# Linear attention and two expert layers on one core: scores and values by key halves on four array tiles

## The chip, the cores and the metric

The kernel runs on one core of a Trainium2 chip. The metric is the time of one execution in device microseconds (us). The kernel before takes 1233.74 us, the median of three runs (1233.2 to 1234.08).

## The reference

Three stages follow each other on 3072 tokens (4 batches of 768) with 384 features.

```python
for t in range(S):                       # H = 8 heads of D = 48, S = 768
    state = alpha[:, :, t, :, None] * state + einsum('bhd,bhe->bhde', k[:, :, t], v[:, :, t])
    y[:, :, t] = einsum('bhd,bhde->bhe', q[:, :, t], state)
x = y as (tokens, 384)
h = x @ w_in                             # 384 -> 2048
x = where(h > 0, h, exp(min(h, 0)) - 1) @ w_out
p = domain_probs / (domain_probs.sum(-1) + 1e-9)
for e in range(4):                       # 384 -> 1024 -> 384
    out += p[:, e:e+1] * (relu(x @ w1[e]) @ w2[e])
```

## The kernel before

The attention is computed in chunks of C = 128 tokens; six chunks of four batches make 24 **units** (chunk, batch). With P the running product of the decays inside a chunk, q is multiplied by P and k by 1/P; the scores are then k times q, masked to the causal triangle, and the values are v times masked scores plus the state of the chunks before. A unit has these parts, each a function: `prep0` (the product P by a scan on VectorE, its logarithm and inverse on ScalarE), `prep1` (a Newton step for the inverse, which also scales k), `prep2` (scales q), `scores` (L439, and the masks L447 on VectorE), `ktrans` (four transposes of k, L460), `yout_t` (the states' share L485 and the values L490, then `pack`), `state` (the new state, L521 and two steps of VectorE) and `xtrans` (y into the operand x0 of the next layer, as a high and a low part: L547 on ScalarE, L548 on VectorE).

The heads stand two by two: head h uses the partitions 64 (h % 2) to 64 (h % 2) + 48 of `raw`, so two heads use the upper and the lower half of the array's rows (two **row tiles**). Scores have 128 columns of weights, so they run as two tiles. In L485 the weights are 64 wide and the output goes to partitions 0 or 64, so there are two **column tiles** as well, and four heads are in flight. In L490 the contraction is over all 128 keys and the output over 48 of 64 partitions: two column tiles. `pack` copies the two banks of y to SBUF (L499), and six small DMAs (L505) then move the last two heads' rows, 16 partitions each, to where the next layer wants them.

The first expert layer works on **items** (chunk, f), 16 for each chunk, 96 in all. An item has two halves of nine matmuls each: `first` computes 128 hidden features for 512 tokens (L620), and `second` feeds those of the item two before into three output banks (L645). Between them VectorE and ScalarE apply the activation: two activations of ScalarE (L629, L630), L631 on VectorE, a copy of ScalarE (L636) and L637 on VectorE. Behind each half a list `slots` places one step of a unit (and one of the weight preparation for the last layer, L547, L548, L673): the attention of chunk c runs during the items of chunk c - 1. The 24 steps of a chunk's four units are spread over 26 halves.

Work on other engines that depends on a half is put on a queue with `later` and issued by the next `flush`, of which there is one in each half. PE, ScalarE, VectorE and GpSimd run in exactly this order, SP's DMAs in an order that the scheduler sets. In each unit the steps come as

```python
s = [scores + ktrans], [prep0 of the next], [prep1 of the next], [xtrans of the one before],
    [yout_t + state], [prep2 of the next]
```

PSUM has eight banks. `a0` and `a1` serve scores and values in turn (`abank`), `h0` to `h2` the first halves, the transposes and the new states in turn (`hbank`), `t0` to `t2` the second halves. Chunks 1 and 2 run in a prologue with an order of its own and in the first items; the last layer (L924 on) begins at about 500 us.

## Time and profile before

| | |
|---|---|
| median of three runs | 1233.74 us (1233.2 to 1234.08) |
| the profiled execution | 1234.16 us |
| its span | 1232.5 us, 17874 instructions, mean granted clock 0.998 |
| PE busy | 1219.7 us (99%) |
| VectorE busy | 869.0 us (71%) |
| ScalarE busy | 592.8 us (48%) |
| GpSimd busy | 492.5 us (40%) |

A matmul's end is modelled, so busy PE is read as "PE was not idle", and the cost of a part is read from one start to the next. A wait behind a row in brackets is the idle time of the engine before it and what ended it. PEld is TensorE's weight load, which overlaps its matmuls.

### The profile page before, as it was taken

Reading aid. Unit: us, or ns where it says so; the run is one execution under the profiler, and the core shown is the slowest. Engines: PE = TensorE matmul, PEld = TensorE weight load, DVE = VectorE, ACT = ScalarE, POOL = GpSimd, SP = SyncE. Lnnn points to the kernel's source line nnn. Section 1 sums busy time; section 2 is a strip of 40 time slices with the busy share of each in tenths; the row PEclk is TensorE's granted clock in tenths of the full one; section 3 lists DMA queues with packets and bytes.
Section 4 is the critical chain, followed back from the end, with each engine's and each line's share of the span. In section 5 each row is a group of like instructions: output and inputs, shape, how many; then the busy total and the mean of one; then the engine's idle time right before and its main releaser. Section 6 shows DMA issues by size and latency. Waiting matters only on the chain.

```text
span 1232.5 us, 17874 instructions
## 1 busy us (share of the span) xinstructions
PE 1219.7 (99%) x6475; PEld 994.3 (81%) x6475; DVE 869.0 (71%) x1433; ACT 592.8 (48%) x1092; POOL 492.5 (40%) x388
## 2 busy tenths in 40 slices
PE   8999999999999999999999999999999999999997
PEld 5788888888887888788888888888888888888886
DVE  8996877777777678657576757575766576667664
ACT  6886566667666567434334333433433333342331
POOL 2000000000000000377688847867977474546662
PEclk9999999999999999999999999999999999999999
DMA  9632555555546467536556578654645874344331
GB/s 375 218 111 90 185 183 182 183 189 197 187 157 221 144 218 261 197 137 233 190 179 227 214 270 311 235 212 154 242 185 215 327 252 167 120 158 167 108 128 62
DMA packets 64816, 239.93 MB, mean 195 GB/s; under 512 B 7640, under 2 KB 33464, under 8 KB 55376
## 3 DMA queue, kind: packets, MB, share of 16 engines
q1 hardware_dynamic: 63856, 233.99, 52.9%
q10 hardware_dynamic: 864, 4.72, 1.0%
q8 instruction: 53, 0.87, 0.3%
q14 instruction: 43, 0.35, 0.1%
HBM read 178.27 MB, written 59.42 MB: 193 GB/s over the span
## 4 chain that ended last, share of the span: by engine, by line
PE 94%; DVE 4%; ACT 1%; DMA 0%; issue 0%; SPq 0%; ACTq 0%; DVEq 0%
PE h L924 27%; PE t L971 16%; PE t L645 16%; PE h L620 15%; PE a L971 11%; PE h L971 5%; PE a L439 2%; PE a L490 2%; PE a L485 1%; PE h L460 1%; PE h L521 1%; DMA raw<-in_att_dram 0%; DVE s_s L263 0%; DVE cv L93 0%; DVE s_p L220 0%
## 5 line engine op out<-in xcount | busy, mean ns | idle before, releaser
L944 POOL TENSOR_TENSOR u<-u 128x512 f32<-128x512 f32 x66 | 97.4, 1475 | 583.4 <-DMA pb<-pd 484.2
L924 PE MATMUL h<-xc_Q,wa 128*128 128x512 f32 x780 | 219.0, 390 | 0.2
L645 PE MATMUL t<-g,w_W 128*128 128x512 f32 x864 | 215.4, 393 | 0.0
L620 PE MATMUL h<-x,w_W 128*128 128x512 f32 x864 | 214.0, 392 | 1.2 <-DVE g L637 0.7
L899 ACT ACTIVATE g_W<-c 128x512 fp32r<-128x512 f32 x128 | 80.6, 630 | 276.4 <-DVE c L944 266.9
L944 DVE TENSOR_TENSOR u<-h,u 128x512 f32<-128x512 f32 x225 | 154.8, 688 | 80.8 <-PE h L924 79.8
L902 POOL TENSOR_TENSOR g_W<-c,g_W 128x512 fp32r<-128x512 f32 x128 | 165.5, 1301 | 77.1 <-ACT c L900 73.0
L620 PEld LDWEIGHTS h<-x,w_W 128*128 128x128 f32 x864 | 160.6, 188 | 35.8 <-DVE g L637 1.2
L645 PEld LDWEIGHTS t<-g,w_W 128*128 128x128 f32 x864 | 160.3, 188 | 33.9 <-issue 0.4
L924 PEld LDWEIGHTS h<-xc_Q,wa 128*128 128x128 f32 x780 | 145.9, 188 | 32.1 <-DVE c L944 0.8
L971 PE MATMUL t<-g_W,wb 128*128 128x512 f32 x576 | 157.5, 389 | 0.0
L900 ACT ACTIVATE c<-c 128x512 f32<-128x512 f32 x192 | 121.5, 633 | 12.2
L971 PEld LDWEIGHTS t<-g_W,wb 128*128 128x128 f32 x576 | 108.1, 188 | 22.5
L944 DVE TENSOR_TENSOR c<-u,h 128x512 f32<-128x512 f32 x123 | 84.2, 685 | 45.3 <-PE h L924 44.9
L631 DVE SCALAR_TENSOR_TENSOR h<-e,h 128x512 f32<-128x512 f32 x96 | 66.6, 693 | 66.1 <-ACT e L630 65.9
L938 DVE COPY u<-h 128x512 f32<-128x512 f32 x99 | 68.3, 691 | 59.2 <-PE h L924 59.1
L924 PE MATMUL h<-xc_W,wa 128*128 128x512 f32 x390 | 109.5, 389 | 0.0
L971 PE MATMUL a<-g_W,wb 128*128 128x512 f32 x384 | 108.2, 389 | 0.0
L899 ACT ACTIVATE g_X<-c 128x512 fp32r<-128x512 f32 x64 | 40.3, 629 | 132.1 <-DVE c L944 125.5
L902 POOL TENSOR_TENSOR g_X<-c,g_X 128x512 fp32r<-128x512 f32 x64 | 82.8, 1305 | 39.6 <-ACT c L900 35.5
L924 PEld LDWEIGHTS h<-xc_W,wa 128*128 128x128 f32 x390 | 73.0, 188 | 15.6 <-DVE u L944 0.4
L629 ACT ACTIVATE e<-h 128x512 f32<-128x512 f32 x96 | 57.2, 595 | 56.1 <-PE h L620 54.8
(162 smaller groups left out, 1789.0 us busy)
## 6 DMA issues: line engine op xcount, KB each, us to landing
wa<-wad SPq DMA_DIRECT2D x33, 1536.0 KB, 6.4
wb<-wbd SPq DMA_DIRECT2D x30, 1536.0 KB, 7.4
raw<-in_att_dram SPq DMA_DIRECT2D x22, 964.0 KB, 6.2
wad<-wh SPq DMA_DIRECT2D x44, 384.0 KB, 2.8
wbd<-wh SPq DMA_DIRECT2D x43, 384.0 KB, 3.3
xcd<-xh SPq DMA_DIRECT2D x30, 512.0 KB, 2.9
wraw<-in_we_dram SPq DMA_DIRECT2D x20, 576.0 KB, 4.4
xc_Q<-xcd SPq DMA_DIRECT2D x6, 1536.0 KB, 7.6
```

The costliest lines, as they stand in the source:

```text
L439: nc.tensor.matmul(ps[j][:, a * C:(a + 1) * C], raw[r, K0 + a * C:K0 + (a + 1) * C], raw[r, Q0 + a * C:Q0 + (a + 1) * C], start=True, stop ...
L620: nc.tensor.matmul(h[:, 0:n], w[:, wl, fi, k * 128:(k + 1) * 128], x[:, xl, k, n0:n0 + n], start=((k, wl, xl) == TERMS[0]), stop=((k, wl, ...
L629: nc.scalar.activation(out=e, in_=h, func=AF.Relu, scale=-1.0)
L631: return lambda: nc.vector.scalar_tensor_tensor(out=h, in0=e, scalar=-1.0, in1=h, op0=ALU.add, op1=ALU.max)
L645: nc.tensor.matmul(self.xa[k][:, 0:n], w[:, wl, fi, DM + k * 128:DM + (k + 1) * 128], g[:, gl, 0:n], start=(first and i == 0), stop=(last ...
L899: nc.scalar.activation(out=g[:, n, 0], in_=v, func=AF.Relu)
L900: nc.scalar.activation(out=v, in_=v, func=AF.Relu)
L902: lambda: nc.gpsimd.tensor_tensor(out=g[:, n, 1], in0=v, in1=g[:, n, 0].bitcast(F32), op=ALU.subtract)
L924: nc.tensor.matmul(b, w[:, wl], x[:, xl], start=(j == 0), stop=(j == 2))
L938: nc.vector.tensor_copy(out, b)
L944: (nc.vector if "b" in (a0, a1) or dst == "S5" else nc.gpsimd).tensor_tensor(out=out, in0=val(a0, b), in1=val(a1, b), op=ALU.add if op == ...
L971: nc.tensor.matmul(oa[m, d], wt[:, f, wl, d * 128:(d + 1) * 128], G[m][:, f, gl], start=first, stop=last)
```

## The change

From chunk 3 on (`TURNED = 2` counts chunks from 0), so for 16 of the 24 units:

- **Scores** are computed by halves of 64 keys. The early half meets all 128 queries, the late half only the last 64, since the others are masked away. Each matmul has 64 columns of weights, so four tiles are in use. In every second pair of heads the halves of k are exchanged (by the Newton step, which writes them so) and with them those of v (on the host), so that the two pairs of a round use different column tiles.
- **Masks**: three operations for each bank instead of one, into two tiles `smt` whose never-written corners are zeroed once by `begin_turned` on GpSimd, together with a second mask for the exchanged order.
- **Values** contract over 64 keys at a time, on four tiles. Row tile 0 writes bank `ps[0]`, row tile 1 `ps[1]`, the states' share as well; each head has a part in both. `pack` copies the first bank (one copy by ScalarE) and `total`, one flush later, adds the second on VectorE; the six DMAs start behind it.
- **Order** of a unit's steps: scores, transposes; prep0 and xtrans; prep1; values and state; prep2; an empty step.
- For all chunks `swap`, which gives the column tile of a head, follows another rule, with the rows of w_in exchanged to match, and `norm_probs` is spread over three items.

```diff
-    return h ^ (h // 2 % 2)
+    return h ^ ((h // 2 ^ h // 4) % 2)
...
+            kp = l if u[0] >= TURNED else k
             nc.vector.tensor_tensor(out=t, in0=P, in1=rP, op=ALU.mult)
-            nc.vector.tensor_tensor(out=k, in0=k, in1=rP, op=ALU.mult)
-            nc.vector.scalar_tensor_tensor(
-                out=k, in0=t, scalar=2.0, in1=k, op0=ALU.subtract, op1=ALU.mult, reverse0=True
-            )
+            nc.vector.tensor_tensor(out=kp, in0=k, in1=rP, op=ALU.mult)
+            parts = [(k, t, kp)]
+            if u[0] >= TURNED:
+                o, t, kp = (v.rearrange("p (a n) t -> p a n t", n=2) for v in (k, t, kp))
+                lo, hi = slice(0, 64), slice(64, C)
+                parts = [(o[:, :, 0], t[:, :, 0], kp[:, :, 0])]
+                parts += [(o[:, :, 1, i], t[:, :, 1, j], kp[:, :, 1, j]) for i, j in ((hi, lo), (lo, hi))]
+            for out, t, kp in parts:
+                nc.vector.scalar_tensor_tensor(
+                    out=out, in0=t, scalar=2.0, in1=kp, op0=ALU.subtract, op1=ALU.mult, reverse0=True
+                )
...
+        for a0 in (0, 2):
+            for late in range(2):
+                for a in (a0, a0 + 1):
+                    n, q = 64 * (late ^ a % 2), a * C + 64 * late
+                    for j in range(2):
+                        r = slice(64 * j, 64 * j + D)
+                        nc.tensor.matmul(
+                            ps[j][n:n + 64, q:(a + 1) * C], raw[r, K0 + a * C + n:K0 + a * C + n + 64],
+                            raw[r, Q0 + q:Q0 + (a + 1) * C], start=True, stop=True,
+                        )
...
+                for v in (
+                    (slice(0, 128), slice(None), slice(None), slice(64, C)),
+                    (slice(0, 64), slice(None), 0, slice(0, 64)),
+                    (slice(64, 128), slice(None), 1, slice(0, 64)),
+                ):
+                    nc.vector.tensor_tensor(out=o[v], in0=s[v], in1=m[v], op=ALU.mult)
...
+            if apart:
+                return ps[row][r:r + n, h // 2 * C:(h // 2 + 1) * C]
...
+            for late, order in enumerate((range(H), (0, 3, 4, 7, 1, 2, 5, 6))):
+                for h in order:
+                    row = late ^ h // 2 % 2
+                    other = row != h % 2
+                    r, q = slice(64 * row, 64 * row + 64), 64 * late * (not other)
+                    n = 64 if other and not swap(h) % 2 else D
+                    nc.tensor.matmul(
+                        to(h, n, row)[:, q:C], raw[r, V0 + h * D:V0 + h * D + n],
+                        self.sm[u, h % 2][r, h // 2, q:C], start=False, stop=True, skip_group_check=True,
+                    )
...
+            def total():
+                nc.vector.tensor_tensor(out=y[0:SW], in0=ps[1][0:SW], in1=y[0:SW], op=ALU.add)
+                spread()
+
+            if apart:
+                nc.scalar.copy(y[0:SW], ps[0][0:SW])
+                self.later(total)
...
+        if u[0] >= TURNED:
+            s[1:] = [s[1] + s[3], s[2], s[4], s[5], []]
...
-        at(F1 + 2, self.norm_probs)
+        for n in range(3):
+            at(F1 + n, self.norm_probs, n)
```

The line numbers move: L439 becomes L498 (scores), L447 becomes L514 (masks), L460 L523, L485 L552, L490 L563, L521 L611, L620 L712, L645 L737, L631 L723, L637 L729, L419 L450, L429 L460 (the product for q), L529 and L530 L619 and L620, L548 L638, L673 L765; the sum of the two banks is L586. In the rows of the order below the third word on names output and input tiles (`a` the score and value banks, `h` and `t` the layer's, `smt` and `sm` masked scores, `wc`, `ut` and `wh` the weight preparation) and the size of the output.

PE, the scores of the first unit of chunk 4, before and then in the change (the first nine of 17 rows there):

```order
L439 MATMUL a_2132<-raw 128x128
L439 MATMUL a_2133<-raw 128x128
L439 MATMUL a_2132<-raw 128x128
L439 MATMUL a_2133<-raw 128x128
L439 MATMUL a_2132<-raw 128x128
L439 MATMUL a_2133<-raw 128x128
L439 MATMUL a_2132<-raw 128x128
L439 MATMUL a_2133<-raw 128x128
L460 MATMUL h_2142<-ident,raw 128x128 x4
```

```order
L498 MATMUL a_2222<-raw 64x128
L498 MATMUL a_2223<-raw 64x128
L498 MATMUL a_2222<-raw 64x128
L498 MATMUL a_2223<-raw 64x128
L498 MATMUL a_2222<-raw 64x64
L498 MATMUL a_2223<-raw 64x64
L498 MATMUL a_2222<-raw 64x64
L498 MATMUL a_2223<-raw 64x64
L498 MATMUL a_2222<-raw 64x128
```

Eight matmuls of 128 rows and 128 columns of output become sixteen of 64 rows, four with 128 columns and four with 64 in turn.

PE, the same unit's states and values, before and then in the change (from the last row of the states):

```order
L485 MATMUL a_2233<-raw,st_146 64x128 x2
L485 MATMUL a_2234<-raw,st_146 64x128 x2
L485 MATMUL a_2233<-raw,st_146 64x128 x2
L485 MATMUL a_2234<-raw,st_146 64x128 x2
L490 MATMUL a_2233<-sm,raw 48x128 x2
L490 MATMUL a_2234<-sm,raw 48x128 x2
L490 MATMUL a_2233<-sm,raw 48x128 x2
L490 MATMUL a_2234<-sm,raw 48x128 x2
L521 MATMUL h_2251<-raw,kn 64x48 x8
```

```order
L552 MATMUL a_2316<-raw,st_146 64x128
L563 MATMUL a_2315<-smt,raw 48x128 x2
L563 MATMUL a_2316<-smt,raw 48x128 x2
L563 MATMUL a_2315<-smt,raw 48x128
L563 MATMUL a_2315<-smt,raw 64x128
L563 MATMUL a_2316<-smt,raw 64x128
L563 MATMUL a_2316<-smt,raw 48x128
L563 MATMUL a_2316<-smt,raw 64x128
L563 MATMUL a_2315<-smt,raw 64x128
L563 MATMUL a_2316<-smt,raw 48x128
L563 MATMUL a_2315<-smt,raw 48x128
L563 MATMUL a_2316<-smt,raw 48x64
```

Eight values of 128 columns become sixteen; the last four have 64 columns (the first of them is shown). The states stay eight.

VectorE, the same unit, from the last Newton step to the sum's place, before and then in the change:

```order
L419 SCALAR_TENSOR_TENSOR raw<-nt,raw 128x512
L637 TENSOR_TENSOR g<-h_2176,g 128x512
L548 TENSOR_TENSOR wh<-wc,wh 128x3x128
L673 TENSOR_TENSOR ut<-wraw 128x128
L673 TENSOR_TENSOR ut<-ut,wraw 128x128
L673 TENSOR_TENSOR wc<-ut,wraw 128x256
L673 TENSOR_TENSOR wc<-wc,wraw 128x128 x2
L631 SCALAR_TENSOR_TENSOR h_2215<-e,h_2215 128x512
L529 TENSOR_TENSOR tmp<-h_2251,st_146 128x192
L530 TENSOR_TENSOR st_146<-tmp,P 128x4x48
L429 TENSOR_TENSOR raw<-raw,P 128x512
L673 TENSOR_TENSOR wc<-wraw 128x256
```

```order
L450 SCALAR_TENSOR_TENSOR raw<-nt,lnP 128x2x64 x2
L729 TENSOR_TENSOR g<-h_2276,g 128x512
L638 TENSOR_TENSOR wh<-wc,wh 128x3x128
L619 TENSOR_TENSOR tmp<-h_2341,st_146 128x192
L620 TENSOR_TENSOR st_146<-tmp,P 128x4x48
L460 TENSOR_TENSOR raw<-raw,P 128x512
L765 TENSOR_TENSOR ut<-wraw 128x128
L765 TENSOR_TENSOR ut<-ut,wraw 128x128
L765 TENSOR_TENSOR wc<-ut,wraw 128x256
L765 TENSOR_TENSOR wc<-wc,wraw 128x128 x2
L723 SCALAR_TENSOR_TENSOR h_2352<-e,h_2352 128x512
L586 TENSOR_TENSOR yt<-a_2316,yt 112x512
```

The two steps of the state (`tmp`, `st`) and the product for q (`raw<-raw,P`) stood behind the activation's step of the item (L631) and stand ahead of it now (L723); the sum of the banks (L586) is new and stands right behind that step.

## Rows read from the trace of the kernel before

**Rows 1.** The page, busy us of each engine, share of the span, instructions

```profile
PE 1219.7 (99%) x6475; PEld 994.3 (81%) x6475; DVE 869.0 (71%) x1433; ACT 592.8 (48%) x1092; POOL 492.5 (40%) x388
```

**Rows 2.** Windows: stretch: length, busy (x instructions) by engine, clock, DMA share, GB/s

```profile
124.00:495.00 371.00, 370.76 (x2365) 301.54 (x2366) 281.57 (x552) 242.50 (x508) 0.00 (x0) 1.00 0.56 193
...
193.50:262.60 69.10, 69.10 (x507) 56.09 (x507) 53.84 (x105) 46.09 (x99) 0.00 (x0) 1.00 0.55 189
```

**Rows 3.** Timeline, PE, a unit of chunk 4: start us, length us, engine, line, operation

```profile
195.67 1.16 PE L439 MATMUL a<-raw 48*128 48x128 f32 x16
196.77 0.66 PE L460 MATMUL h<-ident,raw 128*128 128x128 f32 x4
...
205.55 0.67 PE L485 MATMUL a<-raw,st 48*64 48x128 f32 x16
206.14 1.08 PE L490 MATMUL a<-sm,raw 128*48 128x128 f32 x16
207.06 0.62 PE L521 MATMUL h<-raw,kn 128*64 128x48 f32 x16
...
209.79 2.21 PE L620 MATMUL h<-x,w_W 128*128 128x512 f32 x9
211.93 1.16 PE L439 MATMUL a<-raw 48*128 48x128 f32 x16
```

**Rows 4.** Windows with one start, L485 alone: (x) counts records that have started

```profile
205.50:205.73 0.23, 0.18 (x8) 0.18 (x12) 1.00 0.00 0
...
205.50:205.84 0.34, 0.29 (x12) 0.29 (x16) 1.00 0.00 0
```

**Rows 5.** The same for L521

```profile
207.00:207.11 0.11, 0.06 (x4) 0.11 (x4) 1.00 0.00 0
...
207.00:207.17 0.17, 0.12 (x6) 0.17 (x6) 1.00 0.00 0
```

**Rows 6.** Timeline, PE, a unit of the last chunk

```profile
367.76 0.67 PE L485 MATMUL a<-raw,st 48*64 48x128 f32 x16
...
369.37 0.50 PE L645 MATMUL t<-g,w_W 128*128 128x512 f32 x1
```

**Rows 7.** Groups by form, VectorE, 193.5 to 262.6: busy us, mean ns, idle before

```profile
L631 DVE SCALAR_TENSOR_TENSOR h<-e,h 128x512 f32<-128x512 f32 x14 | 9.7, 694 | 12.2 <-ACT e L630 12.2
...
L447 DVE TENSOR_TENSOR sm<-a,mask 128x512 f32<-128x512 f32 x8 | 5.1, 682 | 0.0
...
L673 DVE TENSOR_TENSOR wc<-wc,wraw 128x128 f32<-128x128 f32 x6 | 1.8, 292 | 0.2
...
L673 DVE TENSOR_TENSOR wc<-wraw 128x256 f32<-128x256 f32 x2 | 0.8, 418 | 0.0
```

**Rows 8.** Timeline, VectorE, the same unit

```profile
203.94 0.70 DVE L631 SCALAR_TENSOR_TENSOR h<-e,h 128x512 f32<-128x512 f32 x1 [2.31 <-ACT e L630]
...
206.47 0.68 DVE L637 TENSOR_TENSOR g<-h,g 128x512 fp32r<-128x512 f32 x1
...
207.54 0.28 DVE L673 TENSOR_TENSOR ut<-wraw 128x128 f32<-128x128 f32 x1
...
209.18 0.69 DVE L631 SCALAR_TENSOR_TENSOR h<-e,h 128x512 f32<-128x512 f32 x1
209.78 0.35 DVE L529 TENSOR_TENSOR tmp<-h,st 128x192 f32<-128x192 f32 x1
...
210.44 0.69 DVE L429 TENSOR_TENSOR raw<-raw,P 128x512 f32<-128x512 f32 x1
```

**Rows 9.** Timeline, SP, the copies inside y; the view of tile yt

```profile
209.24 4.05 SPq L505 DMA_DIRECT2D yt<-yt  x6
...
DMA to landing us min/median/max: 1.7/2.1/7.1
```

**Rows 10.** Timeline, ScalarE, the same unit

```profile
200.61 0.63 ACT L402 ACTIVATE lnP<-P 128x512 f32<-128x512 f32 x1 [2.08 <-DVE P L395]
...
202.66 0.58 ACT L629 ACTIVATE e<-h 128x512 f32<-128x512 f32 x1
```

More of the change, by code (lines that the diff above doesn't have):

```diff
@@ L37 @@
 LISTED = 5
+TURNED = 2
 SW = 64 + D
@@ L160, in consts @@
         make_identity(nc, self.ident)
-        self.mask = const.tile([128, 128], mybir.dt.bfloat16, name="mask")
-        nc.gpsimd.memset(self.mask, 1.0)
+        self.masks = const.tile([128, 2, 128], mybir.dt.bfloat16, name="mask")
+        self.mask = self.masks[:, 0]
+        nc.gpsimd.memset(self.masks, 1.0)
         nc.gpsimd.affine_select(
@@ L173, in consts, with begin_turned @@
             self.st.append(s)
+    def begin_turned(self):
+        m = self.masks[:, 1]
+        for v, base in ((m[:, 0:64], 64), (m[0:64, 64:128], 0)):
+            self.nc.gpsimd.affine_select(
+                out=v, in_=v, compare_op=ALU.is_ge, fill=0.0, base=base, pattern=[[1, 64]], channel_multiplier=-1,
+            )
+        self.smt = []
+        for j in range(2):
+            t = self.ap.tile([128, NP, C], F32, tag="sm", name="smt", bufs=2)
+            v = t.rearrange("p (a n) t -> p a n t", n=2)
+            self.nc.gpsimd.memset(v[64:128, :, 0, 0:64], 0.0)
+            self.nc.gpsimd.memset(v[0:64, :, 1, 0:64], 0.0)
+            self.smt.append(t)
     def warm(self, n, tag):
@@ L356, in load_probs, with norm_probs @@
         self.nc.sync.dma_start(out=self.pr, in_=self.probs)
-    def norm_probs(self):
+    def norm_probs(self, part):
         nc = self.nc
         p = self.pr
-        s = self.wp.tile([128, 256], F32, tag="wt", name="psum_e")[0:NCH * B, 0:C]
-        nc.vector.tensor_tensor(out=s, in0=p[:, 0], in1=p[:, 1], op=ALU.add)
-        for e in range(2, NE):
-            nc.vector.tensor_tensor(out=s, in0=s, in1=p[:, e], op=ALU.add)
-        nc.vector.tensor_scalar_add(s, s, 1e-9)
-        nc.vector.reciprocal(s, s)
+        if part == 0:
+            self.prs = self.wp.tile([128, 256], F32, tag="wt", name="psum_e")[0:NCH * B, 0:C]
+        s = self.prs
+        if part == 0:
+            nc.vector.tensor_tensor(out=s, in0=p[:, 0], in1=p[:, 1], op=ALU.add)
+            for e in range(2, NE):
+                nc.vector.tensor_tensor(out=s, in0=s, in1=p[:, e], op=ALU.add)
+            return
+        if part == 1:
+            nc.vector.tensor_scalar_add(s, s, 1e-9)
+            nc.vector.reciprocal(s, s)
+            return
         nc.vector.tensor_tensor(out=p, in0=p, in1=s.unsqueeze(1).to_broadcast([NCH * B, NE, C]), op=ALU.mult)
@@ L1203, in run @@
                 do(s)
+            if i == TURNED * F1 - F1 - 1:
+                self.begin_turned()
             for f, a in post.pop(i, []):
@@ L1427, in _layout @@
     att[:, :, :, A0:V0] = decay.reshape(NCH, B, 128, V0 - A0)
-    att[:, :, :, V0:] = v.reshape(B, H, NCH, C, D).transpose(2, 0, 3, 1, 4).reshape(NCH, B, C, DM)
+    x = v.reshape(B, H, NCH, C, D).transpose(2, 0, 3, 1, 4).copy()
+    for h in range(H):
+        if h // 2 % 2:
+            x[TURNED:, :, :, h] = np.roll(x[TURNED:, :, :, h], C // 2, axis=2)
+    att[:, :, :, V0:] = x.reshape(NCH, B, C, DM)
     def pair(a, b, f):
```

62 lines of the change are left out of this document (41 added, 21 removed).

## The prediction, made before the changed kernel was run

> **What bounds the kernel now.** I read the page first: TensorE is busy for 1219.7 us, 99% of the span [rows 1]. The windows of the stretch that the change touches say more: from 124 to 495 us PE works 370.76 of 371.00 us, and in the dense part of chunk 4, where its four units stand, 69.10 of 69.10 us, at the full granted clock (1.00), while VectorE works 53.84 us and ScalarE 46.09 us [rows 2]. So in this stretch a matmul step removed is time removed, as long as VectorE and ScalarE keep up. The timeline of PE shows what one unit costs there [rows 3]: scores (L439) from 195.67 to the transposes (L460) at 196.77, 1.10 us; later states (L485) from 205.55 to 206.14, 0.59, and values (L490) to the new state (L521) at 207.06, 0.92. Between them stand halves of an item, nine matmuls each.
>
> Each f32 matmul is two records. How many run side by side is seen by counting what has started by a given moment. Of L485, 8 records by 205.73 and 12 by 205.84 [rows 4]: a **step** of four array tiles takes 0.11 us with 128 columns. Of L521, 4 by 207.11 and 6 by 207.17 [rows 5]: a step of two tiles with 48 columns and 64-wide weights takes 0.06. L439 is 16 records on two tiles: 8 steps of 0.11 and 0.2 for going into and out of its array shape. L485 is 4 steps of 0.11 and 0.15 for that.
>
> **The change, part by part.** Scores: 16 matmuls, 32 records on four tiles, so 8 steps, four of 128 columns and four of 64. The four-tile step with 64 columns is in no row. Half the columns of a 0.11 step would be 0.055; from above it is bounded by 0.11 itself. I take 0.06, the step of L521, which is nearest in columns and has weights of the same width. Scores become 4 x 0.11 + 4 x 0.06 + 0.15 = 0.83 us, 0.26 less. At the bound of 0.11 they would be 1.03, 0.06 less.
>
> States and values: both on 64x64 tiles now, so the change of array shape between them goes and one before L521 comes. States stay 4 steps; values are 16 matmuls, 8 steps: four of 128 columns for the halves in `range(H)`, two of 128 and two of 64 for the others. 10 x 0.11 + 2 x 0.06 + 0.15 = 1.37 us against 0.59 + 0.92 = 1.51 today. L521 loses its overlapped start; the same entry into a shape costs about 0.06, so 0.08 is left (at 64 columns for 0.11: 0.02 more than today). In the last chunk nothing like L521 follows, and L485 with L490 takes 369.37 - 367.76 = 1.61 us [rows 6]: 0.24 less (0.14 at the bound).
>
> Over 16 units: 16 x 0.26 + 12 x 0.08 + 4 x 0.24 = 4.2 + 1.0 + 1.0 = **6.2 us less on PE**; at the bound 1.3 us.
>
> A bank for each row tile: I give it nothing. In the states of today heads 0 and 1 write one bank from both row halves, and still all four tiles start within one 0.11 step [rows 4]. The Trainium skill (TensorEngine Tiling (Array Packing), Gotcha 1: PSUM Pressure) says that different row tiles cannot access the same bank at once. By that rule the states would run in twice the steps now and would gain 4 x 0.11 us in each unit, 7 us in all; the trace shows the four steps already, so the sum goes without it. The separate bank matters here only because both key halves of a head write the same partitions.
>
> VectorE: a mask of 128x512 (0.682 us) becomes one of 128x256 (0.42) and two of 128 columns (0.29 each, taken from 128x128) [rows 7]: +0.32, twice in a unit. The last Newton step (an operation and size like L631's, 0.69) is split in the same three: +0.31. The sum of the two banks is new, 112x512 out of PSUM, 0.68 like L447. Together +1.63 us a unit, 26 us in all. ScalarE has one copy of 512 columns for two of 256, a little less. In the dense part of a chunk VectorE goes from 53.84 to about 60.4 us in 67.7: 89%. What hides it are its waits for ScalarE before L631, 12.2 us of its 15.3 idle [rows 2, 7]. And there is room behind: the L637 at 206.47 ends at 207.15, and the bank it frees is taken by the L620 at 209.79 [rows 3, 8].
>
> The new order: values come one half earlier, the sum is queued on VectorE two flushes behind them, and the next unit's scores need the bank that the sum reads. I follow units 1 to 2 of chunk 4, where they stand closest (six halves). Today scores start at 195.67, the following L631 at 203.94 (8.3 later), the one after it at 209.18 (5.24 more), the next scores at 211.93 (16.26 later) [rows 3, 8]. After: the first of these L631 comes 0.64 later (two masks), at 8.9. Between it and the next stand Newton (+0.31), the two of the state (209.78 to 210.44, 0.66) and the product for q (some 0.6), which stood behind it: 5.24 + 1.57 = 6.8, so 15.7. Then 0.6 to the sum (209.18 to 209.78 is that step behind L631) and 0.69 for it: done at 17.0. PE is there at 16.26 - 0.26 - 0.08 = 15.9. **Scores wait 1.1 us.** In the other chunks the five L673 of weight preparation (207.54 to 209.18, 1.64 us [rows 8]) stand elsewhere in the order, and the sum is done about 0.5 before it is wanted; in the last, where PE has no transposes and no state, about 0.3 after. 1.4 us in all. From unit 2 on the distance is a half more, or the sum stands in the flush after.
>
> The six small DMAs of y now start after the sum, not after ScalarE's copies. Their issue takes 4.05 us on SP and landing 2.1 [rows 9]: at 17.0 + 6.2 = 23.2, 6.2 after the (late) scores. But the copy of y into x stands two steps earlier than before, and ScalarE reaches it after two activations and the copy of the transposes, each like L402 (0.63 [rows 10]), some 2.2 after the scores. It waits about 4 us, and behind it stand a cast, the three activations of the decay (L402 at 200.61 to L629 at 202.66, 2.05 [rows 10]) and the next item's activations. L631 of that item comes about 1.7 later than in the unit before, its L637 ends around 13.9, and the bank is wanted at 13.8. I put 0.25 us a chunk on this, 1.0 in all. On SP the stores of weights and the next load of raw queue behind those DMAs; they have a chunk's time.
>
> At nothing: the selects and fills of `begin_turned` on GpSimd, which does nothing between 124 and 495 us [rows 2]; the three pieces of `norm_probs`; the swapped rows of w_in. If the fills came late, the first masks would wait for them once.
>
> **Sum.** 6.2 less, 1.4 + 1.0 back: **3.8 us less**. The profiled execution took 1234.16 us (span 1232.5), 0.4 above the median of the three runs; it would be 1230.4 (span 1228.7), and the median **1229.9 us**.
>
> **The rivals.** (a) *Short steps cost as long ones.* Four weight loads and four matmuls may set the pace of a step, and 64 columns take 0.11. Then PE gains 1.3 us; the waits shrink to about 1.6, since PE comes later; the time is 1234.0. For it: no row shows four tiles with 64 columns. Against it: L521 does two tiles in 0.06, and the four starts of an L485 step already lie within 0.11 with the streaming. The Trainium skill (TensorEngine Tiling (Array Packing), Instruction Overhead) gives some 60 cycles for each matmul and warns against tiling a dimension that is small already; were it paid four times in a step this would be the result, and the steps of L485 speak against that.
>
> (b) *No new waits.* VectorE fills its waits and the sum is always early: 1227.5.
>
> (c) *VectorE becomes the bound.* The place is the pair of L631 and L637 in the dense parts: the 12.2 us of waits for ScalarE are set by when PE ends a half, and if they don't shrink, the added 6.5 us of a chunk push every later result. It decides from 1.55 us of the 6.5 in a chunk (a quarter) reaching PE; then the 6.2 are gone. At half of it, 4 x 3.25 = 13.0, the time is 1233.7 + 6.8 = 1240.5. For it: 89% on an engine that works in order, and ScalarE's wait for y in the same places. Against it: the 2.6 us of room above, and that PE waits for nothing there now.
>
> (d) *Fours do not form.* If the new matmuls ran two by two, scores would take 8 x 0.11 + 8 x 0.06 + 0.15 = 1.51 (+0.41), and states with values 12 x 0.11 + 4 x 0.11 + 4 x 0.06 + 0.15 = 2.15 (+0.64): 16 x 1.05 = 17 us more, 1250. Against it: today's L485, issued in the same order of tiles, forms them.
>
> **How the numbers follow.** Two runs of this kernel can be told apart from about 0.2%, 2.5 us: faster is below 1231.3, slower above 1236.2. The forecast with waits between 1 and 3.7 us (1228.5 to 1231.2): 0.48. (b): 0.15. (a): 0.14. Waits like (c) that eat the gain without turning it (1231.3 to 1236): 0.10. (c) proper: 0.10. (d): 0.03. Faster 0.63, same 0.24, slower 0.13. For 8 in 10 the range reaches from just under (b), 1227.2, to past (a), 1235.
>
> **What would show it.** Scores between 0.80 and 0.86 us from their first start to the transposes, states with values 1.35 to 1.40; the count of started records rising by four in 0.06 in the short steps. VectorE's sum ending after PE has reached the second unit's scores in chunk 4, by about 1 us, and not in chunk 3. A wait of ScalarE of some 4 us for y in the second unit of each chunk. Wrong would be short steps of 0.11, or idle PE before L620 or L645 all through the dense parts.

## The result, and the profile after

The changed kernel takes **1246.3 us** (median of six runs, 1244.8 to 1249.0) where the kernel before takes 1233.9: 1.0104 times as long, 95% interval [1.0094, 1.0115]. It is 1% slower; the forecast was 1229.9 us, in a range that ended at 1235.0. One run of the kernel before took 3157 us, and the ratio, which is of the means of the other runs, leaves it out. The profiled execution took 1249.01 us (span 1247.3), 2.8 above the median, so its waits are not quite those of the median run. Further down "after" is this kernel. In its profile L498 are the scores, L523 the transposes, L552 and L563 states and values, L611 the new state, L712 and L737 the network (L620 and L645 before), L586 the sum, L580 y's small copies, L637 and L638 the high and low parts of a split (x's among them), L723 and L729 VectorE's two steps of the network, L758 the load of weights.

The page after (busy us of each engine; the chain that ended last, by engine; the group of L712 with the idle time before it), and the chain by engine from the page before:

```profile
PE 1219.8 (98%) x6987; PEld 992.1 (80%) x6987; DVE 890.6 (71%) x1545; ACT 589.9 (47%) x1076; POOL 494.8 (40%) x394
...
PE 76%; DVE 12%; ACT 5%; DMA 3%; SPq 2%; issue 2%; ACTq 0%; DVEq 0%
...
L712 PE MATMUL h<-x,w_W 128*128 128x512 f32 x864 | 215.2, 393 | 10.4 <-DVE g L729 8.2
```

```profile
PE 94%; DVE 4%; ACT 1%; DMA 0%; issue 0%; SPq 0%; ACTq 0%; DVEq 0%
```

VectorE has 21.6 us more than in [rows 1] (26 were forecast), and the chain that ended last now runs through VectorE, ScalarE, DMAs and SP for 22% of the span, where it was 5%. On PE itself the change did what was computed. The timeline of PE, a unit of chunk 5, answers to [rows 3]:

```profile
286.48 0.90 PE L498 MATMUL a<-raw 48*64 48x128 f32 x32
287.31 0.66 PE L523 MATMUL h<-ident,raw 128*128 128x128 f32 x4
...
294.05 0.67 PE L552 MATMUL a<-raw,st 48*64 48x128 f32 x16
294.54 0.95 PE L563 MATMUL a<-smt,raw 64*48 64x128 f32 x32
295.41 0.67 PE L611 MATMUL h<-raw,kn 128*64 128x48 f32 x16
```

Scores take 287.31 - 286.48 = 0.83 us (1.10 before), states and values 295.41 - 294.05 = 1.36 (1.51 before). How fast the short steps go is read as in [rows 4], from windows with one start on L498 alone (the first bracket counts records that have started):

```profile
286.40:286.70 0.30, 0.23 (x8) 0.23 (x12) 1.00 0.00 0
286.40:286.82 0.42, 0.34 (x15) 0.35 (x19) 1.00 0.00 0
```

Seven of the eight records of the two short steps start within 0.12 us: 0.06 a step. But PE now waits. What the engines waited for, from 110 to 460 us (us in total, times, longest):

```profile
ACT x L637 <- DMA yt<-yt: 37.2, 12, 6.5
...
DVE wc L765 <- DMA wraw<-in_we_dram: 8.3, 3, 4.4
...
PE h L712 <- DVE g L729: 7.4, 4, 3.4
...
PEld a L498 <- DVE yt L586: 5.4, 7, 1.5
```

The first of these rows is new in its size (4.3 us in the kernel before, 9.2 in e1_order_only below). The place that the prediction followed, units 1 to 2 of chunk 4, in the timelines of VectorE, PE, SP and ScalarE:

```profile
216.72 0.68 DVE L586 TENSOR_TENSOR yt<-a,yt 112x512 f32<-112x512 f32 x1
...
200.50 0.90 PE L498 MATMUL a<-raw 48*64 48x128 f32 x32
...
216.41 0.43 PE L498 MATMUL a<-raw 48*64 48x128 f32 x2
217.46 0.89 PE L498 MATMUL a<-raw 48*64 48x128 f32 x30 [0.62 <-DVE yt L586]
...
217.24 0.38 SPq L758 DMA_DIRECT2D wraw<-in_we_dram  x1
217.71 4.54 SPq L580 DMA_DIRECT2D yt<-yt  x6
...
223.77 0.51 ACT L637 CAST x<-yt 128x384 fp32r<-128x384 f32 x1 [3.81 <-DMA yt<-yt]
```

Scores of unit 1 started at 200.50, so the sum ends 16.9 us later (forecast 17.0), the next scores are there at 15.9 (forecast 15.9; all but their first two records wait for the sum), and ScalarE stands 3.8 us for y (forecast about 4). What followed from that was far larger than the forecast.

### The profile page after: what moved, and what is told of

Same layout as the page of the kernel before. It is cut to its first block, busy times and chain, and to the rows that moved or that the text cites. A ratio compares the mean times of both kernels' runs of the same rounds, so it can differ in the third digit from the quotient of the medians.

```text
span 1247.3 us, 19035 instructions
## 1 busy us (share of the span) xinstructions
PE 1219.8 (98%) x6987; PEld 992.1 (80%) x6987; DVE 890.6 (71%) x1545; ACT 589.9 (47%) x1076; POOL 494.8 (40%) x394
## 4 chain that ended last, share of the span: by engine, by line
PE 76%; DVE 12%; ACT 5%; DMA 3%; SPq 2%; issue 2%; ACTq 0%; DVEq 0%
PE h L1016 26%; PE t L1063 15%; PE a L1063 10%; PE h L712 8%; PE t L737 8%; PE h L1063 5%; DVE h L723 2%; SPq L580 1%; DVE smt L514 1%; ACT e L722 1%; DVE g L729 1%; DVE wh L638 1%; ACT e L721 1%; DMA yt<-yt 1%; DVE wc L765 1%
## 5 line engine op out<-in xcount | busy, mean ns | idle before, releaser
L712 PE MATMUL h<-x,w_W 128*128 128x512 f32 x864 | 215.2, 393 | 10.4 <-DVE g L729 8.2
L737 PE MATMUL t<-g,w_W 128*128 128x512 f32 x864 | 215.9, 393 | 0.8 <-DVE g L729 0.8
L712 PEld LDWEIGHTS h<-x,w_W 128*128 128x128 f32 x864 | 160.0, 188 | 47.4 <-DVE g L729 11.2
L737 PEld LDWEIGHTS t<-g,w_W 128*128 128x128 f32 x864 | 160.2, 188 | 35.0 <-DVE g L729 1.2
L723 DVE SCALAR_TENSOR_TENSOR h<-e,h 128x512 f32<-128x512 f32 x96 | 66.5, 693 | 47.5 <-ACT e L722 47.0
L729 DVE TENSOR_TENSOR g<-h,g 128x512 fp32r<-128x512 f32 x96 | 66.0, 688 | 33.3 <-ACT g L728 33.0
```

Source lines behind the costliest of these rows:

```text
L712: nc.tensor.matmul(h[:, 0:n], w[:, wl, fi, k * 128:(k + 1) * 128], x[:, xl, k, n0:n0 + n], start=((k, wl, xl) == TERMS[0]), stop=((k, wl, ...
L723: return lambda: nc.vector.scalar_tensor_tensor(out=h, in0=e, scalar=-1.0, in1=h, op0=ALU.add, op1=ALU.max)
L729: return g, lambda: nc.vector.tensor_tensor(out=g[:, 1], in0=h, in1=g[:, 0].bitcast(F32), op=ALU.subtract)
L737: nc.tensor.matmul(self.xa[k][:, 0:n], w[:, wl, fi, DM + k * 128:DM + (k + 1) * 128], g[:, gl, 0:n], start=(first and i == 0), stop=(last ...
```

## The experiments

All times are medians. The kernel before was between 1233.2 and 1233.5 us next to each set. "4 to 6" is the time from the first start of the scores of chunk 4 to that of chunk 6 on PE's timeline of each profiled run: two whole chunks (before 162.61, after 171.04). In four of these stretches PE's granted clock fell for a while, which makes them longer: twice in e15, once in e9 and e14, once and for longer in e13; the part on the late sum comes back to this.

| run | what it is | us | ratio to before, 95% | 4 to 6, us |
|---|---|---|---|---|
| e1_order_only | before + new order | 1234.7 | 1.0011 [1.0001, 1.0020] | 162.61 |
| e3_vector_load | before + VectorE's new work | 1234.1 | 1.0004 [0.9994, 1.0013] | 162.60 |
| e4_scores_alone | scores by halves, old values, old order | 1235.1 | 1.0013 [1.0004, 1.0023] | 163.45 |
| e5_scores_new_order | the same, new order | 1230.5 | 0.9975 [0.9964, 0.9986] | 161.63 |
| e6_no_sum | after without the sum | 1228.9 | 0.9963 [0.9949, 0.9977] | 161.06 |
| e7_sum_aside | sum into a tile nobody reads | 1232.4 | 0.9989 [0.9980, 0.9999] | 161.70 |
| e18_copies_ahead | late sum, copies ahead of it | 1239.5 | 1.0049 [1.0032, 1.0066] | 164.50 |
| e2_xtrans_late | after, x two steps later | 1252.7 | 1.0166 [1.0140, 1.0193] | 170.94 |
| e9_two_y_tiles | e2 + second y tile | 1245.7 | 1.0101 [1.0084, 1.0118] | 168.77 |
| e15_x_one_step_later | after, x one step later, second y tile | 1249.5 | 1.0127 [1.0110, 1.0144] | 171.79 |
| e16_copies_own_queue | after, copies on GpSimd's queue | 1249.9 | 1.0128 [1.0111, 1.0145] | 171.35 |
| e17_x_later_own_queue | e15 + copies on GpSimd's queue | 1242.3 | 1.0079 [1.0062, 1.0096] | 165.73 |
| e14_old_order | after, old order | 1243.9 | 1.0079 [1.0063, 1.0096] | 168.62 |
| e13_late_sum_q_by_gpsimd | after, q product by GpSimd | 1243.3 | 1.0071 [1.0054, 1.0088] | 171.09 |
| e8_sum_at_once | after, sum one flush earlier | 1233.8 | 1.0002 [0.9993, 1.0012] | 162.75 |
| e11_at_once_two_tiles | e8 + order of e9, second tile | 1238.6 | 1.0044 [1.0027, 1.0061] | 165.32 |
| e10_q_by_gpsimd | e8 + q product by GpSimd | **1229.4** | **0.9967 [0.9956, 0.9979]** | 161.92 |
| e12_scores_q_by_gpsimd | e5 + q product by GpSimd | 1230.1 | 0.9974 [0.9964, 0.9984] | 161.94 |

### One part of the change at a time

The first four runs were to tell three theories apart: A, ScalarE stands in order for y's small copies; B, VectorE has too much to do; C, the new order itself costs the time.

**e1_order_only**, the new order on the kernel before:

```diff
         s.append(N(self.prep2))
+        if u[0] >= 2:
+            s[1:] = [s[1] + s[3], s[2], s[4], s[5], []]
```

> The kernel before with the new order of a unit's steps alone (chunks 3 to 6); tiles, masks and y as before. Theory A (ScalarE stands waiting for the small copies of y, which start late and are wanted two steps earlier): y starts here without the sum, some 5 us earlier than in the changed kernel, so ScalarE waits little: 1234 to 1238. Theory B (VectorE has too much to do): nothing is added to VectorE, 1233 to 1235. Theory C (the order itself: state's steps and the product for q ahead of the activation): 1240 or more.

**e3_vector_load**, the kernel before with the mask and the last Newton step in three pieces each, and one idle 112x512 addition a unit behind the copies of y:

```diff
+                parts = [(al, slice(0, C))] if u[0] < 2 else [(al, hi), (slice(0, 2), lo), (slice(2, 4), lo)]
+                for x, y in parts:
+                    nc.vector.tensor_tensor(out=sm[:, x, y], in0=s[:, x, y], in1=m[:, x, y], op=ALU.mult)
```

> The kernel before with VectorE's added work alone: each mask and the last Newton step in three pieces of the same total size, and an addition of 112x512 in each unit one flush after y is packed, on a tile that nobody else uses; order, tiles and y as before. Theory A: 1233 to 1236. Theory B: 1240 to 1250. Theory C: 1233 to 1236.

Neither the order nor VectorE's 1.63 us a unit costs anything worth the name alone: 1234.7 and 1234.1, and the two chunks take 162.6 us in both, as before. That ends C, and B as a cause by itself.

**e4_scores_alone**, the changed kernel with the old values, y's way and order:

```diff
-        apart = c >= TURNED
+        apart = False
...
-        if u[0] >= TURNED:
-            s[1:] = [s[1] + s[3], s[2], s[4], s[5], []]
```

> The changed kernel with the scores by key halves alone: values over all 128 keys in two banks as before, no sum of banks, the old order of steps. PE loses 0.26 us a unit, 4.2 us in all; VectorE has 0.95 us a unit more instead of 1.63. Theory A: no wait for y is added, 1229 to 1231. Theory B: half of the load remains and costs more than the gain, 1236 or more. Theory C: 1229 to 1231.

1235.1, against the 1229 to 1231 that stood for it: the shorter scores won nothing. PE waits ahead of them instead; the timelines of VectorE and of PE at one such wait:

```profile
164.64 0.69 DVE L460 TENSOR_TENSOR raw<-raw,P 128x512 f32<-128x512 f32 x1
...
165.43 0.90 PE L498 MATMUL a<-raw 48*64 48x128 f32 x32 [1.46 <-ACT wh L637]
```

ScalarE's cast is named as releaser, but it had long been done; what ends at 165.33 is the q product (L460), and the scores start 0.1 later, as they do in six of the 16 units. In the old order that product stands right ahead of the scores, and VectorE comes to it later by the pieces that the change adds. If so, the new order, which puts it a step earlier, must take the wait away. **e5_scores_new_order** keeps the second half of the edit out (`apart = False` alone):

> Scores by key halves and the new order of steps; values and y's way (two copies by ScalarE, the six small copies right behind them) as before. In e4_scores_alone the scores' steps were 0.25 us per unit shorter, but in five units the first of them started 0.05 to 0.1 us after VectorE's q product of that unit ended, and PE had stood 0.6 to 1.9 us for it. Theory Q (scores alone lost because the q product stood right ahead of them, and the new order, which puts it a step earlier, takes that wait away): 1228.5 to 1231.0 us. Rival: the halves themselves (more steps, more VectorE pieces of the mask and of the keys) hold the rest back wherever the q product stands: 1233.5 to 1237 us.

1230.5, as theory Q had it. So the halved scores are worth 3 us of their 4.2, once the q product is out of their way; the change of order, worth nothing alone, is what makes them pay.

### The sum

**e2_xtrans_late**, the changed kernel with x's part of the unit before two steps later:

```diff
-            s[1:] = [s[1] + s[3], s[2], s[4], s[5], []]
+            s[1:] = [s[1], s[2], s[3] + s[4], s[5], []]
```

> The changed kernel with y's copy into x two steps later, ahead of the values in the same step. Theory A: the 33 us of ScalarE's waits for y go nearly whole, and with them most of PE's idle time; about 1228 to 1233. Theory B: VectorE's work is the same, so 1241 or more. Theory C: the rest of the order is the same, so 1238 or more.

1252.7, a miss for A. ScalarE's wait for the small copies fell from 37.2 to 3.9 us, and another took its place (waits from 110 to 460 us):

```profile
ACT yt L590 <- DVE x L638: 28.7, 10, 4.5
...
PE a L498 <- DVE yt L586: 7.5, 6, 2.4
```

There is one y tile, and the next unit's copy into it now waits until VectorE has taken x's low part out of the old one. Three kernels then take the sum out, put it aside and put it earlier. The first two leave the second bank's half out of the result, so they are probes and not versions. **e6_no_sum**:

```diff
                 nc.scalar.copy(y[0:SW], ps[0][0:SW])
-                self.later(total)
+                spread()
```

> The changed kernel without VectorE's sum of the two banks: y is ScalarE's copy of the first bank alone, and the six small copies are issued right behind it, so the second bank's half of the values is computed and left out of the result. Theory Y (what was lost is y's way: bank, sum on VectorE, six copies, ScalarE's and VectorE's parts of x, and only then the next unit's copy into the one y tile): 1224 to 1229 us. Rival H (the values' steps by halves, or the order with both, hold PE back for another reason): 1238 us or more.

**e7_sum_aside**, the sum back at its place, for nobody:

```diff
-                nc.vector.tensor_tensor(out=y[0:SW], in0=ps[1][0:SW], in1=y[0:SW], op=ALU.add)
-                spread()
+                nc.vector.tensor_tensor(out=self.zz[0:SW], in0=ps[1][0:SW], in1=self.zz[0:SW], op=ALU.add)
...
                 nc.scalar.copy(y[0:SW], ps[0][0:SW])
+                spread()
                 self.later(total)
```

> As e6_no_sum, with VectorE's sum of the same size at its place in VectorE's row, but into a tile that nobody reads: VectorE's load and the time for which the second bank is held are those of the changed kernel, only y's way is short; y is the first bank's half alone. Theory Y (latency of y): within 2 us of e6_no_sum, 1225 to 1231 us. Rival V (the banks that the sum holds, which the next scores need, or VectorE's load on top of the other pieces): 1238 us or more.

**e8_sum_at_once**, the result whole, the sum queued with ScalarE's copy and not one flush behind it:

```diff
                 nc.scalar.copy(y[0:SW], ps[0][0:SW])
-                self.later(total)
+                total()
```

> The changed kernel, its result unchanged, with the sum put into VectorE's row in the same half item as ScalarE's copy, five to six rows earlier (ahead of the state's two operations, the q product and the network's next two). Theory Y: y is whole some 3 to 4 us earlier, and ScalarE's waits of 2 to 6 us for the small copies mostly go: 1228 to 1236 us. Rival: VectorE, in order, now stands for ScalarE's copy itself, and the network's operations behind it are late by as much: 1242 us or more.

e6: 1228.9 (at the upper end of what theory Y expected), e7: 1232.4 (1.4 above its range, but far from rival V's 1238), e8: 1233.8, within its range. The added addition, its place in VectorE's row and the bank that it holds cost 3.5 us (e7 against e6), and the same addition with y behind it 17.4 (after against e6). Queued one flush earlier it costs 4.9. In the place shown above e8's sum, its q product and the next scores read

```profile
208.73 0.69 DVE L586 TENSOR_TENSOR yt<-a,yt 112x512 f32<-112x512 f32 x1
...
210.00 0.69 DVE L460 TENSOR_TENSOR raw<-raw,P 128x512 f32<-128x512 f32 x1
...
211.87 0.90 PE L498 MATMUL a<-raw 48*64 48x128 f32 x32
```

with the scores of unit 1 at 195.96: the sum starts 12.8 us after them (16.2 in the changed kernel), and ScalarE's waits for y are 9.3 us in all.

### By which way the late sum acts

The chain of waits in the changed kernel, 125 to 160 us (start, length, what), in the first unit of chunk 3:

```profile
133.14 0.58 SPq L580
...
138.13 3.96 DMA wraw<-in_we_dram
...
142.60 0.69 DVE h L723
```

SP's timeline there, of the kernel before and then of the changed one, with the sum from VectorE's:

```profile
126.87 3.68 SPq L505 DMA_DIRECT2D yt<-yt  x6
...
131.46 2.31 SPq L666 DMA_DIRECT2D wraw<-in_we_dram  x2
```

```profile
127.92 0.69 DVE L586 TENSOR_TENSOR yt<-a,yt 112x512 f32<-112x512 f32 x1
...
132.04 0.38 SPq L758 DMA_DIRECT2D wraw<-in_we_dram  x1
132.58 3.68 SPq L580 DMA_DIRECT2D yt<-yt  x6
136.35 0.50 SPq L392 DMA_DIRECT2D pd<-p  x1
138.13 0.39 SPq L758 DMA_DIRECT2D wraw<-in_we_dram  x1
```

Before, y's copies go out first and both loads of weights behind them. After, the sum was whole at 128.61, but a load of weights stands ahead of the copies, and its queue waits 8.7 us there until the store of x1 (`x1raw`, like this load in a tile with the tag `stg`) has left the staging tile; the copies leave 4 us late, the second load behind them at 138.13, and VectorE stands for its weights until 142.1. SP's wait for that store is in the changed kernel

```profile
SPq L758 <- DMA x1d<-x1raw: 20.1, 3, 8.7
```

and 2.3 us, once, in the kernel before. So three ways lay open: ScalarE standing for y, SP's order, and VectorE's row with the banks it holds.

**e9_two_y_tiles** (`bufs=2` for y on e2's order):

> The order of e2_xtrans_late (x's part of the unit before stands a step later) on the changed kernel, with a second tile for y. In e2_xtrans_late ScalarE's waits for the small copies were gone (3.9 us in place of 37.2), but it stood 28.7 us at the next unit's copy of the bank until VectorE had taken x's low part out of the one y tile. Theory Y (y's way is a loop closed by the one tile): with the second tile that wait goes too, and what is left is the bank that the late sum holds (9 us of scores' waits in e2): 1232 to 1240 us. Rival: the stall is not in y's way at all: 1247 us or more, as in e2.

**e15_x_one_step_later** (`s[1:] = [s[1], s[2] + s[3], s[4], s[5], []]` and `bufs=2`):

> The changed kernel with its late sum, a second y tile, and x's part of the unit before moved by one step only, to the step of the Newton product, not into that of the values as in e2 and e9. Theory Y: the small copies have landed when ScalarE comes to x (under 15 us of waits), VectorE's row is not crowded behind the values: 1233 to 1239 us. Theory R (late sum and crowded row hold the scores whatever ScalarE does): 1243 us or more.

**e16_copies_own_queue** and **e17_x_later_own_queue**, on after and on e15:

```diff
-                        nc.sync.dma_start(
+                        (nc.gpsimd if apart else nc.sync).dma_start(
```

> The changed kernel, its late sum kept, with y's six small copies of chunks 3 to 6 issued by GpSimd's queue in place of SP's. In the changed kernel's trace SP stands 8.7, 3.5 and 7.8 us at a load of weights (for the store that reads the same staging tile) with y's copies behind it, and the next loads of weights stand behind the copies, so that VectorE waits 4.4 us for them. Theory S (the late sum put y's copies behind that load on SP, and later loads behind the copies; SP's order is the loss): 1231 to 1238 us. Theory Y (ScalarE stands for a y whose sum is late, whatever queue copies it): 1241 us or more. Between the two, both have a part.

> e15_x_one_step_later (late sum, second y tile, x's part a step later, where ScalarE no longer waits for y: 5.7 us) with y's small copies on GpSimd's queue. Theory S: 1231 to 1238 us. Theory R (the late sum in a crowded VectorE row holds the scores' banks and the network's operations; queues and ScalarE's waits only move where it shows): 1244 us or more.

**e18_copies_ahead**:

```diff
             def total():
-                nc.vector.tensor_tensor(out=y[0:SW], in0=ps[1][0:SW], in1=y[0:SW], op=ALU.add)
-                spread()
+                for r in (slice(0, D), slice(64, SW)):
+                    nc.vector.tensor_tensor(out=y[r, 0:DM], in0=ps[1][r, 0:DM], in1=y[r, 0:DM], op=ALU.add)
...
                 nc.scalar.copy(y[0:SW], ps[0][0:SW])
+                spread()
                 self.later(total)
```

> The changed kernel with its sum as late as before, but only over the first three pairs' columns and in two operations (the rows that the small copies fill stand between), and the six copies issued on SP right behind ScalarE's copy of the first bank, ahead of the sum: the fourth pair and the spread rows lack the second bank's half. VectorE has some 0.4 us per unit more. y is whole 3 to 8 us earlier than in the changed kernel because the copies no longer follow the sum, and SP's row is that of the kernel before. Theory S, and Y too: 1231 to 1237 us. Theory R: 1243 us or more.

e9: 1245.7, 7 us better than e2 and outside both ranges: the second tile takes ScalarE's wait for it away and most of e2's loss stays. e15: 1249.5, against Y: ScalarE's waits for y are down to

```profile
ACT x L637 <- DMA yt<-yt: 5.7, 2, 3.9
```

and no time is won. e16: 1249.9, against S: SP's row is free of y's copies, VectorE's waits for weights fall from 8.3 to 1.4 us, and no time is won either (from issue to landing the copies take 2.5 us there, median, and 1.8 in the changed kernel). With both, e17: 1242.3, outside both ranges, 4 us below the changed kernel and 7 below either.

Part of this is not waits but PE's clock. PE from 110 to 450 us in the changed kernel, in e15 and in e17, then two stretches of e15 (length, busy us, granted clock, DMA share, GB/s):

```profile
110.00:450.00 340.00, 323.76 (x2684) 1.00 0.50 172
110.00:450.00 340.00, 327.96 (x2680) 0.98 0.49 172
110.00:450.00 340.00, 330.31 (x2719) 1.00 0.52 178
...
142.00:145.50 3.50, 0.96 (x5) 1.00 0.21 86
146.00:149.00 3.00, 3.00 (x8) 0.50 0.33 131
```

```profile
145.59 3.92 PE L712 MATMUL h<-x,w_W 128*128 128x512 f32 x9 [2.63 <-DVE g L729]
149.35 2.24 PE L737 MATMUL t<-g,w_W 128*128 128x512 f32 x9
```

In e15 PE stands still for 12.0 us where it stood 16.2 in the changed kernel, so the wait that was taken away does show. But four times, after PE had stood for 1.8 to 2.6 us, its granted clock fell from 1.00 to 0.50, that is from 2.4 to 1.2 GHz, for 13.6 us in all; nine matmuls of the network took 3.3 to 3.8 us there and take 2.05 at the full clock. From these numbers the lower clock costs e15 an estimated 6.8 us at most. In the profiled runs of the changed kernel, where PE once stood for 3.4 us, and of e17 the clock did not fall there. Chunks 4 and 5 can be compared without it: 171.04 us in the changed kernel, 171.35 in e16 and 165.73 in e17, all at 1.00; of e15's 171.79 an estimated 3.4 are the lower clock of two stretches. So SP's order alone wins nothing, ScalarE's wait alone an estimated 2.7 us, which the clock took back, and both together 5.3.

The profiled runs of e2, e9, e13, e14, e16 and e18 have one to three such stretches too, and the changed kernel's other five runs have a mean granted clock of 0.994 to 0.998, the kernel before 0.998 or 0.999 in nearly all of its runs. From these means an estimated 2.5 us at most of the changed kernel's median are the lower clock. The kernels that come near the kernel before (e6, e7, e8, e10, e12) stay at 0.998 to 0.999.

What remains in e17 is VectorE's part (its waits, PE's weight load on the left):

```profile
PEld a L498 <- DVE yt L586: 5.7, 6, 1.5
...
PEld h L712 <- DVE g L729: 5.1, 4, 1.8
```

e18: 1239.5, between the expectations. With the copies ahead of the sum 6.8 us of the loss are gone. It lies 7.1 above e7, whose sum has the same place in VectorE's row but which no reader of y waits for. That is not a wait of x for the late sum: in e18's trace ScalarE never waits for it (L587 there). Only the scores do, and longer than in e7 (L500, L588), since the sum in two pieces takes 1.11 us instead of 0.68. PE's waits in e18 and then in e7:

```profile
PE a L498 <- DVE yt L587: 5.0, 5, 1.7
...
PE a L500 <- DVE zz L588: 2.1, 3, 1.0
```

From 110 to 450 us PE stands 3.6 us longer than in e7, and two stretches at the lower clock cost an estimated 3.4. So most of the 7.1 us are e18's own, which leaves the copies as the way by which a late y costs most.

**e13_late_sum_q_by_gpsimd** and **e14_old_order** (the two lines of the order taken out):

```diff
-        nc.vector.tensor_tensor(out=q, in0=q, in1=P, op=ALU.mult)
+        (nc.gpsimd if u[0] >= TURNED else nc.vector).tensor_tensor(out=q, in0=q, in1=P, op=ALU.mult)
```

> The changed kernel with its late sum, and the q product of chunks 3 to 6 by GpSimd: VectorE's row is lighter by 0.69 us per unit, by as much as took 4.4 us from e8_sum_at_once. Theory Y (ScalarE's standing for a late y is the loss): ScalarE still waits 25 us or more for the small copies, 1238 to 1246 us. Theory R (VectorE's row running full ahead of the scores is the loss, and the late sum only one more piece of it): 1230 to 1235 us.

> The changed kernel with the old order of steps: x's part of the unit before one step later, the q product last. Theory Y with what e4 showed of the q product: ScalarE waits less for the small copies (under 20 us), and the q product, now behind the sum or next to it, holds the scores: 1244 to 1254 us. Rival (the new order is what lost the time): 1236 us or less.

1243.3: VectorE's row, lighter by 0.69 us a unit, gives back only 3 us while y stays late (ScalarE still waits 35.4 us), as Y had it. 1243.9 for the old order, just below what Y expected: with the late sum the new order costs 2.4 us, where with the old values it gains 4.6 (e5 against e4). It pulls x forward, towards a y that comes later: ScalarE waits 3.9 us for the copies in e14 and 37.2 in the changed kernel.

### A version that beats both

**e10_q_by_gpsimd** is e8 with the edit of e13, **e12_scores_q_by_gpsimd** is e5 with it, **e11_at_once_two_tiles** is e8 with e2's order and the second tile.

> e8_sum_at_once with the q product of chunks 3 to 6 by GpSimd (idle there; a product of this size takes it 1.3 us in a later layer) in place of VectorE's 0.69 us per unit. In e8 the small copies hold ScalarE 9.3 us, no more than without the sum (8.0), yet four network steps are still 1 to 1.5 us late, where VectorE's row has no gap. Theory R (what is left in e8 is VectorE's own row running full for some us): 1229 to 1232.3 us. Rival (VectorE's load does not matter, or both engines slow each other): 1233.3 us or more.

> e5_scores_new_order with the q product of chunks 3 to 6 by GpSimd. In e5 the items of chunks 3 to 6 are 1.4 us longer than in e6_no_sum, most of it the values' own steps and 0.7 us of one late network step. Theory R: 1229.3 to 1230.6 us, the 0.7 us at most. Rival (GpSimd's product, twice as long, comes too late for the scores, or slows VectorE): 1232 us or more.

> e8_sum_at_once with the second y tile and x's part a step later. Theory R (y's way no longer matters in e8): within 1.5 us of e8's 1233.8. Rival (y's way is still what holds e8 back): 1228 to 1231.5 us.

e10: **1229.4 us, 0.9967 [0.9956, 0.9979]**, the whole change with its sum early and the q product on GpSimd; it beats the kernel before by 4 us and the changed one by 17. Its page, and PE's waits ahead of L712 from 110 to 450 us (2.8 us in e8):

```profile
PE 1214.9 (99%) x6983; PEld 991.1 (81%) x6987; DVE 889.6 (72%) x1529; ACT 590.3 (48%) x1076; POOL 513.6 (42%) x410
```

```profile
PE h L712 <- DVE g L729: 0.9, 2, 0.5
```

GpSimd's timeline, the q product in the place shown above:

```profile
199.63 1.20 POOL L460 TENSOR_TENSOR raw<-raw,P 128x512 f32<-128x512 f32 x1 [29.26 <-PE h L712]
```

Theory R's time came, but not by less load: VectorE is busy for 889.6 us here and for 890.1 in e8, since other operations of its row are slowed by GpSimd's (last section). What changed is the place. The q product no longer stands between the sum and the next scores; GpSimd takes it as soon as the decay of that unit is there, 5.8 us behind the scores of unit 1 (at 193.88 here), where VectorE comes to it 14.0 behind them in e8. So the 4.4 us are put down to clearing that stretch. e12: 1230.1, within the expectation; scores alone have little more to win. e11: 1238.6, outside both ranges: moving x later (by two steps, not by the one that the expectation names) costs 4.8 us although ScalarE waits for y only once, 4.0 us. In VectorE's row x's low part and the sum, the state's operations and the q product then stand together, which is the likely cause; it was not tested by itself. It would also make e2 and e9 poor probes: their edit crowded that row while it took a wait away.

## Why the prediction was wrong

**Right: what PE saves.** Scores 0.83 us (forecast 0.83), states and values 1.36 (1.37), short steps 0.06. The 0.06 for L521's lost overlap, for which no row was given, came out at 0.05: from it to the next step 0.55 us before (207.06 to 207.61), 0.60 after (209.46 to 210.06). Rivals (a), short steps as long as long ones, and (d), fours that do not form, fall with these rows. e6, with the new matmuls and no sum, is 4.6 us below the kernel before (1233.5 against 1228.9), of the 6.2 forecast; in its profile the network's weight loads still wait 2.0 us for VectorE. That a bank for each row tile gains nothing was not tried by itself.

**Right as far as it went: VectorE's added work.** It was priced at nothing because ScalarE's waits cover it. On the kernel before it costs nothing (e3). In the changed kernel it is no longer all covered where it stands just ahead of the scores: taking 0.69 us a unit out of that stretch gains 4.4 us (e8 to e10).

**Right in its place, wrong in its number: the scores' wait for the sum.** 1.4 us were forecast, 1.1 of it in chunk 4. The sum's end (16.9 us) and the scores' arrival (15.9) came out to 0.1 us, but the claim that elsewhere it is early did not hold: PE's weight loads waited for L586 seven times, 5.4 us in all, 1.5 the longest. With VectorE's load e7 puts 3.5 us on it.

**The step that failed: the price of a late y.** "I put 0.25 us a chunk on this, 1.0 in all. On SP the stores of weights and the next load of raw queue behind those DMAs; they have a chunk's time." ScalarE's wait was forecast to 4 us in the second unit of each chunk and measured at 3.8 in the place that was followed; but there are twelve such waits, 37.2 us, the longest 6.5. And SP was priced as a queue with room behind the copies: nothing was said of what stands ahead of them once they are issued half an item later. There a load of weights waits up to 8.7 us, and the loads behind the copies make VectorE stand. The waits give back 1246.3 - (1233.9 - 6.2) = 18.6 us, not 2.4. By differences of runs 17.4 us of it belong to the sum: 3.5 the addition and its bank (e7 - e6), and 13.9 more once y waits for it (after - e7), where 1.0 was forecast. Of these 13.9 at least 6.8 come from the six copies behind the sum (after - e18), and an estimated 2.5 at most are PE's lower clock after its waits, a term that the forecast did not have.

These parts are not independent: in chunks 4 and 5 e16 took SP's part away and gained nothing, e15 took ScalarE's and gained an estimated 2.7 us that the clock took back, and e17 took both and gained 5.3. How the rest of e17's loss, 9 us, divides between held banks and a crowded VectorE row was not settled.

**Rival (c)**, VectorE as the bound, had the right sign (1240.5), but its mechanism, added load alone, is not what happened: the load without the sum's lateness is e3, and the same sum one flush earlier is 12.5 us cheaper.

## What to carry to other kernels

An operation put between a result and its readers costs what its place in its engine's row makes it late, not what it takes: the same 0.68 us addition cost 4.9 or 17.4 us for one flush. When a transfer is issued later, look at what stands ahead of it on its queue and not only behind it. An experiment that moves a wait should be read for what it crowds elsewhere, and its granted clock should be looked at before it is said to have won nothing. Two waits can cover each other, so they should also be taken away together.

## What the runs showed of the hardware that was not expected

VectorE stands still while GpSimd's product runs, if its own operation takes both inputs from SBUF. The timelines of GpSimd and VectorE in e10_q_by_gpsimd, chunk 6:

```profile
377.57 1.19 POOL L460 TENSOR_TENSOR raw<-raw,P 128x512 f32<-128x512 f32 x1 [15.30 <-issue]
...
377.47 0.69 DVE L729 TENSOR_TENSOR g<-h,g 128x512 fp32r<-128x512 f32 x1
378.08 1.10 DVE L638 TENSOR_TENSOR wh<-wc,wh 128x384 fp32r<-128x384 f32 x1
379.10 0.55 DVE L638 TENSOR_TENSOR x<-yt,x 128x384 fp32r<-128x384 f32 x1
```

L729, with one input from PSUM, takes its usual 0.69 us. L638, both of whose inputs are in SBUF, takes 1.10 for 0.55: GpSimd ends at 378.76, and 0.42 us later it is done. A 128x128 L765 of 0.29 us takes 1.26 elsewhere. The Trainium skill (SBUF — State Buffer, SBUF: two separate sides) has this rule: an operation of VectorE with two SBUF inputs and one of GpSimd that reads SBUF lock each other out; whichever starts first holds the shared port pair for its whole instruction, and the other fully blocks. The trace agrees with it: 1.10 us for 0.55. Whether e10 would gain more with the product beside operations that read PSUM was not tried.

A wait named after an engine that had long been done was the q product in e4: its end and the scores' start lie 0.1 us apart in six units.
